# A new order of all steps in a kernel that multiplies spectra and gates two mixers

## The chip, the cores and the metric

The kernel runs on one core of a Trainium2 chip. The metric is the device time of one execution in microseconds; the median of several runs counts. Everything is float32.

## What is computed

The inputs are x (1 x 2048 x 512), a complex weight for its two-dimensional real spectrum, and the parameters of a state-space convolution. The reference, cut to what matters:

```python
def _A_ref(x, w_r, w_i):
    X = rfft2(x)
    return irfft2(X * (w_r + 1j * w_i), s=(S, D))

def _B_ref(u, log_A_real, A_imag, C_real, C_imag, log_dt, D_skip):
    dt = exp(log_dt)
    A = -exp(log_A_real) + 1j * A_imag
    C = (C_real + 1j * C_imag) * dt[:, None]
    P = exp((A * dt[:, None])[:, :, None] * arange(L))
    K = 2.0 * einsum("dn,dnl->dl", C, P).real
    y = irfft(rfft(u_t, 2 * L) * rfft(K, 2 * L))[:, :, :L]   # causal convolution
    return y + u * D_skip

g = sigmoid((x * gate_w).sum(-1, keepdims=True))
out = g * _A_ref(x, ...) + (1 - g) * _B_ref(x, ...)
```

For the inputs given, the convolution's kernel is nearly constant along the sequence, so the main path replaces it by a running sum times one number per channel. A branch behind the main path, taken only for other inputs, computes it in full; no step of the change lies in it.

## The kernel before, in words

The Fourier transforms are matrix products in several stages. TensorE (PE) multiplies, and since it writes only PSUM, every product is then moved on by VectorE (DVE) or ScalarE (ACT). GpSimd (POOL) works on SBUF only. The work is cut into named steps of a letter and a number, and the string PLAN writes out the order of all of them by hand. The line `for word in PLAN.split(): todo[word[0]](int(word[1:]))` emits them in that order. Each engine then runs its own steps in the order in which they stand in PLAN, and waits for what a step needs. SyncE (SP) issues nearly all loads and stores in that order too.

The steps, by stage:

- First stage, ten parts of x (0 to 9; 0, 1, 8 and 9 are half as wide). `F` on POOL folds a part (L259: the sum of its two halves). `C` on PE multiplies a part (L276): half u=1 needs x alone, half u=0 needs the fold. `c` on DVE transposes both halves into AR (L284).
- Second stage, eight units of frequencies (0 to 7). Units 1 and 7 are worked in two halves, written 11, 21, 17, 27. `P` on PE (L435), `t` on ACT copies the product out (L440), `D` on PE transforms along channels (L453; units 3 and 5 do part of the next step with extra matmuls, L457), `d` on ACT and `Z` on DVE (L470 to L478) combine even and odd parts. `W` and `U` on DVE multiply by the spectral weights (L490), `l` loads the weights and `L` on ACT patches their first row (L411).
- The complex products are put together on POOL: `p` (L496, L497), then `g` (L509, L510); `h` on ACT patches a row (L517, L518). `I` on PE transforms back along channels (L537), `i` on ACT copies half of it (L543), `V` on DVE writes the sums to AI (L551).
- The running sum for the second mixer: `X` loads x transposed, `x` on ACT copies a half to PSUM (L335), `m` on DVE is the scan (L338), `y` and `o` on ACT scale (L347, L342), and `r` on POOL issues a transfer that adds the one to the other inside SBUF (L352). `k` on PE and `G` make the gate (L375, L385), which goes through DRAM and comes back spread over all partitions with `O`. `H` on POOL multiplies by it (L370). `u` on ACT and `E` on DVE and ACT multiply the gate into the last matrices (L366, L587, L588).
- Last stages: `K0` on PE and `K1` on ACT mend one row of AI (L557, L559), `B` on PE for eight blocks (L571), `b` on DVE transposes (L575), `Q` on PE makes eight blocks of the result (L597), and `q` on DVE adds the second mixer and stores the block (L610, L611). The last block, LASTQ, is added and stored in two halves (L607, L608), one from SP and one from ACT.
- `R`, `T`, `l`, `S`, `J`, `N` are loads of constants and small sums.

PSUM is four buffers (`bufs=4`) of two banks, which all stages share: a step that needs one waits until the buffer it is given has been read for the last time. SBUF has 13 buffers for short-lived blocks, four for weights (also used by the last matrices), three for small copies and four for the running sums and gate rows.

Of the kernel before, what the change touches and what calls it, by code (L numbers as in the profile page):

```python
# [12 lines left out]
ALU = mybir.AluOpType  # L13
AX = mybir.AxisListType

P = 128
# [25 lines left out]
FOLDS = [0, 0, 1, 1, 1, 1, 1, 1, 1, 1]  # L42
ORDER = [8, 9, 0, 1, 10, 2, 11, 3, 12, 4, 13, 5, 14, 6, 15, 7, 16]
_T = np.arange(128)
K2 = np.arange(64).reshape(32, 2).T.ravel()
# [5 lines left out]
def _consts():  # L51
# [44 lines left out]

    s2 = s2.reshape(17, 2, 128, 2, 64)[ORDER].transpose(2, 0, 1, 3, 4)

# [83 lines left out]
def body(ctx: ExitStack, tc: tile.TileContext, x, xg, xt, w, wh, prms, vecs, gw,  # L182
         c_s1e, c_s1f, c_s2e, c_s2, c_s2v, c_s2q, c_s1b, c_s1a, c_s1c, c_dfw, c_zfw, c_dbw, c_pos, c_eye, out):
    nc = tc.nc
    V, G, S, T = nc.vector, nc.gpsimd, nc.scalar, nc.tensor
# [3 lines left out]
    def psum(name):  # L189
        return ps.tile([P, 2, 512], F32, tag="ps", name=name)  # L190
# [21 lines left out]
    s1e, ones = last[:, 0:128], last[:, 128:256]  # L212
# [13 lines left out]
    def blk(shape, name):  # L226
        return work.tile(shape, F32, tag="blk", name=name, bufs=NBLK)
# [4 lines left out]
    t_ = {}  # L232

    with tc.manual_schedule():
# [4 lines left out]
        for k in PARTS:  # L239
            c = slice(128 * k.start, 128 * k.stop)  # L240
# [14 lines left out]
        def fold(q, E):  # L255
            n = 64 * (PARTS[q].stop - PARTS[q].start)
            f = t_["f", q] = blk([P, 2, 512], "f")
            xv = xin(q)
            E.tensor_tensor(f[:, 0, :n], xv[:, 0], xv[:, 1], op=ALU.add)  # L259
            if FOLDS[q] == 2:  # L260
                E.tensor_tensor(f[:, 1, :n], xv[:, 0], xv[:, 1], op=ALU.subtract)


        def C_(q):
            n = 32 * (PARTS[q].stop - PARTS[q].start)
            p = t_["c", q] = [psum("p_s1") for _ in range(2)] if q == LASTC else [psum("p_s1")] * 2
            tiles = [(g, h, slice(64 * h, 64 * h + 64)) for g in range(2) for h in range(2)]
            if FOLDS[q] == 2:
                for g, h, r in tiles:
                    T.matmul(p[0][64 * g:64 * g + 64, h, :2 * n], s1e[r, 0:64], t_["f", q][r, :, g * n:g * n + n], start=True, stop=True, tile_position=(64 * h, 64 * g))  # L270
            else:
                for u in range(1, -1, -1):
                    for i in range(1 if FOLDS[q] > u else 2):
                        for g, h, r in tiles:
                            src = t_["f", q][r, 0] if FOLDS[q] > u else xin(q)[r, i]
                            T.matmul(p[u][64 * g:64 * g + 64, h, u * n:u * n + n], s1e[r, 64 * u * i:64 * u * i + 64], src[:, g * n:g * n + n], start=i == 0, stop=i == 1 or FOLDS[q] > u, tile_position=(64 * h, 64 * g))  # L276

        def c_a(q):
# [3 lines left out]
            for u in range(1, -1, -1):  # L282
                pv = t_["c", q][u][:, :, :2 * n].rearrange("p h (u t c d) -> p u h t c d", u=2, c=16, d=2)
                V.transpose(av[:, u, :, k], pv[:, u])  # L284


        big, sm = few[:, 1:3], few[:, 3]
# [27 lines left out]

        N_ = {0: n0, 1: n1, 2: small, 3: level, 4: n4}


        def new(key, make):
            if key not in t_:  # L320
                t_[key] = make()
            return t_[key]

        def coef(r):
            return (r // 2 % 2) * 2 + r // 4
# [88 lines left out]
        def unit(n):  # L414
            return n % 10, slice(0, P) if n < 10 else slice(64 * (n // 10 - 1), 64 * (n // 10)), range(2) if n < 10 else [n // 10 - 1]
# [76 lines left out]
        def p_a(n):  # L492
            u, r, vs = unit(n)
            t1, t2 = (cut(t_["t", u, k], n).rearrange("p (o i) k -> p o i k", o=2) for k in range(2))
            po = new(("px", u), lambda: blk([P, 2, 2, 2, P], "px")).rearrange("p x a o k -> p x o a k")[..., r]
            G.tensor_tensor(po[:, 0], t1[:, :, 0:4:2], t1[:, :, 1:4:2][:, :, ::-1], op=ALU.subtract)  # L496
            G.tensor_tensor(po[:, 1, :, ::-1], t2[:, :, 0:4:2], t2[:, :, 1:4:2][:, :, ::-1], op=ALU.add)  # L497


        def g_a(n):  # L500
# [89 lines left out]
        def Q_(j):  # L590
            i, k = j // 4, j % 4
            if j == LASTQ:
                p = t_["pq", j] = [psum("p_oa")[:, 0].rearrange("p (b c) -> p b c", b=4) for _ in range(2)]
            else:
                p = t_["pq", j] = psum("p_oa").rearrange("p u (b c) -> p (u b) c", b=4)
            for b in range(8):
                T.matmul((p[b // 4][:, b % 4] if j == LASTQ else p[:, b]).rearrange("p (e c) -> p e c", e=2), VA[:, i, 8 * (k % 2) + b, :, k // 2], s1a[k][:, :, b], start=True, stop=True)  # L597

        def last_a(j, E, p):
            i, k = j // 4, j % 4  # L600
            z, b = k // 2, 8 * (k % 2)
            xv = XT[:, 2 * i:2 * i + 2].rearrange("p e (z c b) -> p e z c b", z=2, b=16)[:, :, z, :, b:b + 8]
            o = AF_[:, 1024 * j:1024 * j + 1024]
            if j == LASTQ:
                for f in range(2):
                    o_ = o[:, 512 * f:512 * f + 512]
                    E.tensor_tensor(o_.rearrange("p (e c b) -> p e c b", e=2, b=4), p[f].rearrange("p b (e c) -> p e c b", e=2), xv[..., 4 * f:4 * f + 4], op=ALU.add)  # L607
                    (nc.sync, nc.scalar)[f].dma_start(out[j, :, 512 * f:512 * f + 512], o_)  # L608
            else:
                E.tensor_tensor(o.rearrange("p (e c b) -> p e c b", e=2, b=8), p.rearrange("p b (e c) -> p e c b", e=2), xv, op=ALU.add)  # L610
                nc.sync.dma_start(out[j], o)  # L611

        def a_a(j):
# [15 lines left out]
        ]  # L629

        todo = {
            "f": lambda q: fold(q, V), "F": lambda q: fold(q, G), "C": C_, "c": c_a, "N": lambda k: N_[k](),
            "X": load_x, "x": x_a, "m": scan, "o": skip, "y": y_a, "z": summed, "r": both, "k": gate, "G": G_, "J": J_, "l": load_w, "L": load_h,
            "P": P_, "t": t_a, "D": D_, "d": d_a, "Z": Z_, "W": lambda u: W_(u, 0, V), "U": lambda u: W_(u, 1, V), "p": p_a, "g": g_a, "h": h_a, "I": I_, "i": i_a, "V": V_,
            "K": K_, "B": B_, "b": b_a, "S": load_a, "O": load_g, "u": near, "Q": Q_, "q": lambda j: last_a(j, V, t_["pq", j]), "a": a_a, "A": lambda j: last_a(j, G, t_["qs", j]),
# [8 lines left out]
    with tc.If(n_small < D):  # L644
        with tc.tile_pool(name="dram", bufs=1, space=bass.MemoryType.DRAM) as dp:
            Kd = dp.tile([D, L], F32, name="Kd")
            with tc.tile_pool(name="kg", bufs=1) as kg:
# [26 lines left out]
                for c in range(0, D, NC):  # L674
# [52 lines left out]
            with tc.tile_pool(name="gx", bufs=1) as gx:  # L727
                s1f = gx.tile([P, 2, P], F32, name="s1g")
                nc.sync.dma_start(s1f, c_s1f)
                for dst, isk in ((KR, True), (AG, False)):  # L730
# [4 lines left out]
                    for h in range(2):  # L735
                        if isk:
# [37 lines left out]
            p = psum("p_sp")  # L774
# [3 lines left out]
            for c in range(16):  # L778
                p = psum("p_gb")
# [20 lines left out]
            for i in range(2):  # L800
# [89 lines left out]
```

## Time and profile before

| | |
|---|---|
| median of 3 runs | 110.65 us (110.46 to 110.81) |
| profiled execution | 110.1 us, span 108.3 us |
| PE busy | 93.2 us (86%) |
| DVE busy | 85.3 us (79%) |
| POOL busy | 75.5 us (70%) |
| ACT busy | 51.5 us (48%) |
| read from and written to DRAM | 19.01 MB, 4.21 MB |

The span goes from the first to the last instruction of one execution on the chip. A row of the timeline gives start, duration, engine, line, operation, tile written and read, and how many such instructions were merged; in brackets stands how long the engine was idle before and what ended that. A row of the groups gives the busy time of all and the mean of one in nanoseconds. PEld is the loading of weights, which overlaps PE; a matmul in float32 counts as two instructions.

### The profile page before, as it was taken

The page shows a single profiled execution, that of the slowest core. Times are in us where ns is not written, and L with a number is a line of the kernel's source. Part 1 is how long each engine was busy: PE and PEld are TensorE (multiplying, and loading weights), DVE is VectorE, ACT ScalarE, POOL GpSimd, SP SyncE. Part 2 cuts the span into 40 slices and gives each one's busy share as a digit, 9 for nine tenths or more (in the row PEclk, how much of TensorE's full clock was granted, in tenths as well). Part 3 has the DMA queues.
Part 4 walks back from the last instruction along what each step waited for, and adds up shares of the span by engine and source line. Part 5 has one row for each costly group of instructions (what it writes and reads, how often), then busy time and mean ns, then how long its engine had stood idle before and what let it go on. Part 6 is the DMA issues. An engine that isn't in the chain of part 4 may idle for free. (4 is left out here: it accounts for less than half of the span.)

```text
span 108.3 us, 2285 instructions
## 1 busy us (share of the span) xinstructions
PE 93.2 (86%) x872; PEld 77.6 (72%) x872; DVE 85.3 (79%) x134; ACT 51.5 (48%) x89; POOL 75.5 (70%) x70
## 2 busy tenths in 40 slices
PE   6899976999997999989899999976699999999200
PEld 6797753999797945368799999966243869999100
DVE  0248989579799788999999999996889979788500
ACT  0000005455749399999796996946870170000000
POOL 0059853222999998599999999999999999700000
PEclk9999999999999999999999999999999999999995
DMA  3999999999999991099978993998325950779950
GB/s 65 373 366 404 397 389 344 382 422 417 427 405 410 417 395 80 0 200 225 191 242 197 254 250 123 273 229 163 95 98 98 189 106 3 312 297 360 393 214 13
DMA packets 8560, 27.67 MB, mean 255 GB/s; under 512 B 968, under 2 KB 1352, under 8 KB 8028
## 3 DMA queue, kind: packets, MB, share of 16 engines
q1 hardware_dynamic: 7132, 22.86, 57.0%
q0 software_dynamic: 1088, 4.19, 20.2%
q10 hardware_dynamic: 320, 0.38, 1.0%
q8 instruction: 9, 0.15, 0.6%
q14 instruction: 11, 0.09, 0.2%
HBM read 19.01 MB, written 4.21 MB: 214 GB/s over the span
## 5 line engine op out<-in xcount | busy, mean ns | idle before, releaser
L490 DVE TENSOR_TENSOR tw<-p_d,w 128x1024 f32<-128x1024 f32 (+1 forms) x20 | 19.3, 1005 | 1.1 <-ACT w L411 0.5
L370 POOL TENSOR_TENSOR XT<-XT,gb 128x1024 f32<-128x1024 f32 x8 | 19.3, 2552 | 0.2 <-DMA XT<-v 0.2
L435 PE MATMUL p_t<-s2e,AR 128*128 128x128 f32 x128 | 16.7, 285 | 2.1 <-DVE AR L284 0.9
L435 PEld LDWEIGHTS p_t<-s2e,AR 128*128 128x128 f32 x128 | 15.7, 196 | 3.4 <-DVE AR L284 1.3
L453 PE MATMUL p_d<-et,dfw 128*128 128x256 f32 (+1 forms) x80 | 16.8, 343 | 0.8 <-ACT v L347 0.3
L537 PE MATMUL p_v<-dbw,gt 128*128 128x128 f32 x128 | 15.2, 276 | 1.6 <-ACT gt L518 1.6
L597 PEld LDWEIGHTS p_oa<-s1a,AR 128*128 128x128 f32 x128 | 15.2, 196 | 1.7 <-ACT s1a L588 0.9
L537 PEld LDWEIGHTS p_v<-dbw,gt 128*128 128x128 f32 x128 | 14.7, 192 | 1.9 <-ACT gt L518 1.8
L597 PE MATMUL p_oa<-s1a,AR 128*128 128x128 f32 x128 | 15.6, 283 | 0.0
L453 PEld LDWEIGHTS p_d<-et,dfw 128*128 128x128 f32 x80 | 12.0, 191 | 3.5 <-ACT gt L517 1.1
L259 POOL TENSOR_TENSOR f<-AI 128x512 f32<-128x512 f32 (+1 forms) x8 | 9.0, 1140 | 7.8 <-DMA AI<-in_x_dram 7.8
L496 POOL TENSOR_TENSOR px<-tw 128x512 f32<-128x512 f32 (+1 forms) x10 | 11.8, 1184 | 2.2 <-DVE tw L490 2.2
L284 DVE STREAM_TRANSPOSE AR<-p_s 128x512 f32<-128x512 f32 (+1 forms) x20 | 10.8, 589 | 2.9 <-PE p_s L276 2.8
L497 POOL TENSOR_TENSOR px<-tw 128x512 f32<-128x512 f32 (+1 forms) x10 | 11.8, 1180 | 0.0
L551 DVE TENSOR_TENSOR AI<-p_v,po 128x512 f32<-128x512 f32 (+1 forms) x20 | 10.4, 577 | 1.3 <-ACT po L543 1.3
L440 ACT COPY et<-p_t 128x1024 f32<-128x1024 f32 (+1 forms) x10 | 8.4, 836 | 6.0 <-PE p_t L435 6.0
L509 POOL TENSOR_TENSOR gt<-px 128x512 f32<-128x512 f32 (+1 forms) x10 | 10.6, 1063 | 0.8
L276 PE MATMUL p_s<-AI,last 64*64 64x128 f32 (+1 forms) x192 | 10.2, 347 | 1.0 <-DMA AI<-in_x_dram 1.0
L510 POOL TENSOR_TENSOR gt<-px 128x512 f32<-128x512 f32 (+1 forms) x10 | 10.6, 1060 | 0.0
L575 DVE STREAM_TRANSPOSE AR<-p_ia 128x1024 f32<-128x1024 f32 x8 | 9.4, 1222 | 1.4 <-PE p_ia L571 1.4
L338 DVE TENSOR_TENSOR_SCAN p_x<-p_x,XT 128x1024 f32<-128x1024 f32 x4 | 9.2, 2293 | 1.3 <-ACT p_x L335 1.3
L610 DVE TENSOR_TENSOR AI<-p_oa,XT 128x1024 f32<-128x1024 f32 x7 | 8.2, 1211 | 1.5 <-PE p_oa L597 1.5
(67 smaller groups left out, 123.0 us busy)
## 6 DMA issues: line engine op xcount, KB each, us to landing
w<-in_w_dram SPq DMA_DIRECT2D x8, 512.0 KB, 7.7
XT<-in_xt_dram SPq DMA_DIRECT2D x4, 1024.0 KB, 8.9
XT<-v POOLq DMA_DIRECT2D x4, 1024.0 KB, 9.9
out_dram<-AI SPq DMA_DIRECT2D x7, 512.0 KB, 3.4
AI<-in_x_dram SPq DMA_DIRECT2D x6, 512.0 KB, 7.7
gb<-gd SPq DMA_DIRECT2D x4, 512.0 KB, 5.2
AI<-in_x_dram SPq DMA_DIRECT2D x4, 256.0 KB, 3.2
s1a<-in_c_s1a_dram SPq DMA_DIRECT2D x4, 256.0 KB, 4.4
```

The lines of the kernel that those rows point to most:

```text
L284: V.transpose(av[:, u, :, k], pv[:, u])
L370: E.tensor_tensor(r, r, t_["gb", h % 2], op=ALU.mult)
L435: T.matmul(cut(p, n, v)[:, 2 * q:2 * q + 2], AR[:, q % 2, 8 * (q // 2) + u, :, v], s2e[:, 2 * u + v], start=True, stop=True)
L453: T.matmul(d[:, o, 1:3] if h else d[:, o, 0:4:3], dfw[:, 2 * h + o], e[:, 2 * h + o], start=True, stop=not z)
L490: E.tensor_tensor(t, z, w, op=ALU.mult)
L496: G.tensor_tensor(po[:, 0], t1[:, :, 0:4:2], t1[:, :, 1:4:2][:, :, ::-1], op=ALU.subtract)
L497: G.tensor_tensor(po[:, 1, :, ::-1], t2[:, :, 0:4:2], t2[:, :, 1:4:2][:, :, ::-1], op=ALU.add)
L509: G.tensor_tensor(gv[:, :, 0], src[0], src[1], op=ALU.subtract)
L510: G.tensor_tensor(gv[:, ::-1, 1], src[0], src[1], op=ALU.add)
L537: T.matmul(p[:, v - vs[0], h, o], rows(u, o, v, h), dbw[:, h, o], start=True, stop=True)
L551: V.tensor_tensor(ai[:, :, :, k], t_["pi", n][:, 0:len(vs), :, 0], t_["po", u][:, v], op=ALU.subtract if k else ALU.add)
L597: T.matmul((p[b // 4][:, b % 4] if j == LASTQ else p[:, b]).rearrange("p (e c) -> p e c", e=2), VA[:, i, 8 * (k % 2) + b, :, k // 2], s1a[ ...
```

## The change

All steps stay, each with its own work, and PLAN is written anew. Code around it changes as far as the new PLAN needs it:

- `C` and `c` are split by halves. `C` and `c` now mean half u=1, the new letters `j` and `w` half u=0, and each half has its place in the order. Only for part 7 do the two halves have PSUM buffers of their own, as before.
- LASTQ, the block that is stored in two halves, is 5 in place of 7.
- `LASTROWS`, `PDVE` and the letter `v` are new and, as set, do nothing.
- The order of units changes. On POOL the products come as 1, 7, 6, 4, 5, 0, 2 and 3 (before: 1, 7, 4, 6, 0, 2, 3, 5), with r1 ahead of p6. The last blocks come as Q0 Q3 Q2 Q1 Q4 Q7 Q6 Q5 (before: Q1 Q0 Q3 Q4 Q2 Q6 Q5 Q7), and the loads, scans, gate steps and stores move with them.

```diff
-LASTQ = 7
-LASTC = 7
+LASTQ = 5
 ...
 PLAN = """
-R7 R0 C1 F2 J0 C0 c1 c0 T0 C2 c2 F3 C3 c3 F4 C4 J1 F5 R1 C5 F6 F8 F9 c4 c5 C6 c6 C8 R9 C9 c8 c9 R6 F7 N1 C7 c7 P11 l1
-P21 l4 t11 t21 N0 N3 D11 d11 D21 d21 Z11 Z21 P17 P27 N4 N2 t17 L1 U11 R5 W11 U21 D17 t27 d17 P4 t4 Z17 l7 W21 L7 U17
-X1 D27 p11 g11 d27 h11 Z27 D4 p21 g21 L4 P6 l0 d4 W17 U27 Z4 W27 p17 P0 U4 R4 g17 p27 W4 X3 X0 g27 t6 h21 P2 L0 t0 p4
-D6 x1 t2 l6 h17 m1 G4 d6 h27 L6 G5 y1 k0 R8 X2 Z6 g4 U6 W6 k1 o3 o2 R10 D0 k2 k3 l2 d0 h4 l5 G1 x2 Z0 W0 D2 U0 L2 d2
-l3 P3 P5 o4 G2 r1 p6 O0 t3 m2 y2 I11 S1 D3 g6 Z2 i11 p0 g0 W2 U2 o5 S0 r2 h6 L5 L3 O1 p2 t5 V11 I17 i17 x0 I6 h0 U3 o0
-g2 V17 I21 i21 W3 D5 i6 S2 m0 y0 p3 g3 h2 V21 V6 O2 I0 o1 W5 I27 r0 U5 p5 g5 i0 i27 h3 x3 H2 o6 V0 I4 i4 V27 m3 I2 V4
-i2 V2 h5 I3 I5 i3 V3 S3 u0 O3 i5 H4 E0 K0 V5 K1 B0 y3 E1 B3 b0 b3 B1 B4 B2 b1 B7 b2 B6 H5 o7 b4 r3 b7 Q1 Q0 u1 b6 B5
-H1 E3 E2 Q3 H0 b5 H3 Q4 q1 q0 H7 H6 q3 Q2 q2 q4 Q6 q6 Q5 Q7 q5 q7
+R7 C0 j0 F2 c0 J0 C1 j1 F3 C2 j2 F4 C3 w0 j3 c1 F5 w1 R0 w2 c2 C4 j4 c3 w3 C5 F6 c4 j5 C6 w4 j6 C7 F8 F9 w5 c5 c6 w6
+c7 F7 C8 C9 j8 c8 j9 c9 w8 w9 j7 w7 P11 J1 N1 T0 R1 P21 t11 t21 D11 d11 D21 N0 R9 R6 N4 N3 d21 Z11 Z21 l1 l7 l4 P17
+P27 t17 L1 U11 U21 W11 R8 W21 D17 t27 d17 L4 Z17 L7 W17 N2 p11 l6 P4 t4 D27 g11 d27 L6 Z27 U17 W27 P6 X1 X0 P5 t6 X2
+x1 t5 D6 k0 k1 p21 g21 h11 h21 d6 m1 y1 U27 D4 Z6 U6 l5 W6 P0 R5 X3 R10 o3 p17 g17 o2 d4 k2 Z4 G4 p27 R4 h17 L5 l0 g27
+G5 h27 t0 x2 r1 k3 D5 G1 p6 g6 G2 l2 h6 o4 I17 W4 U4 D0 m2 p4 g4 W5 i17 V17 L0 o5 l3 U5 p5 P2 d0 y2 x0 t2 h4 Z0 W0 U0
+S2 O2 O0 P3 r2 o0 g5 t3 D2 d2 p0 g0 I11 h5 S0 D3 i11 m0 o1 L2 y0 r0 Z2 V11 I5 W2 I27 U2 L3 p2 W3 i27 U3 S1 V27 p3 g2
+I6 i5 V5 h0 g3 I21 i6 V6 i21 V21 H0 H4 x3 o6 I0 i0 m3 h2 I4 i4 y3 V0 h3 V4 I2 i2 u0 S3 I3 i3 V2 O1 E0 K0 K1 o7 V3 E1
+O3 B0 b0 B1 b1 r3 B3 b3 B2 b2 u1 E2 B7 b7 E3 H1 B6 Q0 b6 H3 H2 B5 B4 Q3 b5 Q2 q0 q3 H5 Q1 H7 b4 H6 Q4 Q7 q2 q1 Q6 q4
+q7 q6 Q5 q5
 """
+APART = (7,)
 ...
-        def C_(q):
+        def C_(q, u):
             n = 32 * (PARTS[q].stop - PARTS[q].start)
...
+            p = new(("c", q, u if q in APART else 0), lambda: psum("p_s1"))
+            for i in range(1 if FOLDS[q] > u else 2):
+                for g in range(2):
+                    for h in range(2):
...
-            "C": C_, "c": c_a,
+            "C": lambda q: C_(q, 1), "j": lambda q: C_(q, 0), "c": lambda q: c_a(q, 1), "w": lambda q: c_a(q, 0),
```

More of the change, by code (lines that the diff above doesn't have):

```diff
@@ L42 @@
 FOLDS = [0, 0, 1, 1, 1, 1, 1, 1, 1, 1]
+APART = (7,)
+LASTROWS = [slice(0, P)]
+PDVE = ()
 ORDER = [8, 9, 0, 1, 10, 2, 11, 3, 12, 4, 13, 5, 14, 6, 15, 7, 16]
@@ L253, in xin, with new, fold, c_a @@
             return X[:, 128 * PARTS[q].start:128 * PARTS[q].stop].rearrange("p (u n) -> p u n", u=2)
-        def fold(q, E):
+        def new(key, make):
+            if key not in t_:
+                t_[key] = make()
+            return t_[key]
+        def fold(q, u, op, E):
             n = 64 * (PARTS[q].stop - PARTS[q].start)
-            f = t_["f", q] = blk([P, 2, 512], "f")
+            f = new(("f", q), lambda: blk([P, 2, 512], "f"))
             xv = xin(q)
-            E.tensor_tensor(f[:, 0, :n], xv[:, 0], xv[:, 1], op=ALU.add)
-            if FOLDS[q] == 2:
-                E.tensor_tensor(f[:, 1, :n], xv[:, 0], xv[:, 1], op=ALU.subtract)
-        def C_(q):
+            E.tensor_tensor(f[:, u, :n], xv[:, 0], xv[:, 1], op=op)
+        def C_(q, u):
             n = 32 * (PARTS[q].stop - PARTS[q].start)
[L266 to L278, printed above, removed]
+            p = new(("c", q, u if q in APART else 0), lambda: psum("p_s1"))
+            for i in range(1 if FOLDS[q] > u else 2):
+                for g in range(2):
+                    for h in range(2):
+                        r = slice(64 * h, 64 * h + 64)
+                        src = t_["f", q][r, u] if FOLDS[q] > u else xin(q)[r, i]
+                        T.matmul(p[64 * g:64 * g + 64, h, u * n:u * n + n], s1e[r, 64 * u * i:64 * u * i + 64], src[:, g * n:g * n + n], start=i == 0, stop=i == 1 or FOLDS[q] > u, tile_position=(64 * h, 64 * g))
+        def c_a(q, u):
             k = PARTS[q]
@@ L281, in c_a @@
             av = AR.rearrange("p u c (h t) d -> p u h t c d", h=2)
-            for u in range(1, -1, -1):
-                pv = t_["c", q][u][:, :, :2 * n].rearrange("p h (u t c d) -> p u h t c d", u=2, c=16, d=2)
-                V.transpose(av[:, u, :, k], pv[:, u])
+            pv = t_["c", q, u if q in APART else 0][:, :, :2 * n].rearrange("p h (u t c d) -> p u h t c d", u=2, c=16, d=2)
+            V.transpose(av[:, u, :, k], pv[:, u])
         big, sm = few[:, 1:3], few[:, 3]
@@ L316, in body @@
         N_ = {0: n0, 1: n1, 2: small, 3: level, 4: n4}
[L319 to L322, printed above, removed]
         def coef(r):
@@ L495, in p_a @@
             po = new(("px", u), lambda: blk([P, 2, 2, 2, P], "px")).rearrange("p x a o k -> p x o a k")[..., r]
-            G.tensor_tensor(po[:, 0], t1[:, :, 0:4:2], t1[:, :, 1:4:2][:, :, ::-1], op=ALU.subtract)
-            G.tensor_tensor(po[:, 1, :, ::-1], t2[:, :, 0:4:2], t2[:, :, 1:4:2][:, :, ::-1], op=ALU.add)
+            E = V if u in PDVE else G
+            E.tensor_tensor(po[:, 0], t1[:, :, 0:4:2], t1[:, :, 1:4:2][:, :, ::-1], op=ALU.subtract)
+            E.tensor_tensor(po[:, 1, :, ::-1], t2[:, :, 0:4:2], t2[:, :, 1:4:2][:, :, ::-1], op=ALU.add)
         def g_a(n):
@@ L607, in last_a @@
                     E.tensor_tensor(o_.rearrange("p (e c b) -> p e c b", e=2, b=4), p[f].rearrange("p b (e c) -> p e c b", e=2), xv[..., 4 * f:4 * f + 4], op=ALU.add)
-                    (nc.sync, nc.scalar)[f].dma_start(out[j, :, 512 * f:512 * f + 512], o_)
+                    for r in LASTROWS:
+                        (nc.sync, nc.scalar)[f].dma_start(out[j, r, 512 * f:512 * f + 512], o_[r])
             else:
@@ L631, in body @@
         todo = {
-            "f": lambda q: fold(q, V), "F": lambda q: fold(q, G), "C": C_, "c": c_a, "N": lambda k: N_[k](),
+            "f": lambda q: fold(q, 1, ALU.subtract, V), "F": lambda q: fold(q, 0, ALU.add, G), "v": lambda q: fold(q, 0, ALU.add, V),
+            "C": lambda q: C_(q, 1), "j": lambda q: C_(q, 0), "c": lambda q: c_a(q, 1), "w": lambda q: c_a(q, 0), "N": lambda k: N_[k](),
             "X": load_x, "x": x_a, "m": scan, "o": skip, "y": y_a, "z": summed, "r": both, "k": gate, "G": G_, "J": J_, "l": load_w, "L": load_h,
```

## The prediction

> **What bounds the kernel now.** I read the page's busy shares first, then the chain that ended last, then the waits, then the timeline by stage. The profiled execution took 110.1 us: a span of 108.3 and 1.8 around it. The median is 110.65, so I work out a difference within the span and take it off the median.
>
> ```profile
> PE 93.2 (86%) x872; PEld 77.6 (72%) x872; DVE 85.3 (79%) x134; ACT 51.5 (48%) x89; POOL 75.5 (70%) x70
> ...
> 74.07 2.06 PE p_v L537 x16
> ...
> 77.90 6.41 PE p_ia L571 x53
> ...
> 89.40 11.52 PE p_oa L597 x96
> ...
> 100.94 0.69 DVE AI L607
> ...
> PE p_v L537 <- ACT gt L518: 1.6, 1, 1.6
> ```
>
> PE is busy 93.2 of 108.3, and 7.4 of the 15.1 idle us lie after its last matmul at 100.92. From 77.90 on it runs without a gap. So the time is B0's start, plus 23.02 of PE work (8 B, 8 Q), plus the tail. B0's start goes back to the last I step, I5, at 74.07. PE had waited 1.6 us for it, the longest PE wait in the kernel, and what it waited for was h5, released by g5 on POOL:
>
> ```profile
> 26.43 0.73 POOL L496 TENSOR_TENSOR px<-tw 128x256 f32<-128x256 f32 x1 [2.19 <-DVE tw L490]
> ...
> 37.24 0.73 POOL L510 TENSOR_TENSOR gt<-px 128x256 f32<-128x256 f32 x1
> ...
> 44.43 1.36 POOL L352 DMA_DIRECT2D XT<-v  x1 [1.40 <-ACT XT L342]
> ...
> 50.91 1.26 POOL L496 TENSOR_TENSOR px<-tw 128x512 f32<-128x512 f32 x1
> ...
> 55.94 1.18 POOL L352 DMA_DIRECT2D XT<-v  x1
> 56.72 1.71 POOL L496 TENSOR_TENSOR px<-tw 128x512 f32<-128x512 f32 x1
> ...
> 72.29 1.28 POOL L510 TENSOR_TENSOR gt<-px 128x512 f32<-128x512 f32 x1
> ```
>
> POOL makes the complex products of all eight units in one string, from p11 at 26.43 to g5's end at 73.57. Its one long wait is 1.40 us, for the ACT work ahead of r1. A whole unit (p and g) takes 50.91 to 55.94, 5.03 us; an r step costs about 1.2 (0.78 from 55.94 to the next p, which then runs 0.45 longer than the 1.26 of the row above). PE has spare time in the middle; POOL's string sets when the last unit can be transformed back.
>
> **Part by part.** The instructions are the same. What moves is their order on every queue, and with it who holds which PSUM buffer.
>
> *First stage: 0.* C and c are planned by halves, so C7's first half, which needs no fold, can fill PE's wait for part 8.
>
> ```profile
> 14.62 2.65 POOL L259 TENSOR_TENSOR f<-AI 128x256 f32<-128x256 f32 x3 [1.54 <-DMA AI<-in_x_dram]
> ...
> 17.33 0.66 PE L276 MATMUL p_s<-f,last 64*64 64x256 f32 x8
> ...
> 18.84 2.15 PE L435 MATMUL p_t<-s2e,AR 128*128 128x128 f32 x16 [0.85 <-DVE AR L284]
> ```
>
> The folds F8, F9, F7 keep their order on POOL and start when part 8 lands (14.62, end 17.27). Half j7 can only follow at 17.33, its transposition after that, and P11 stays at 18.84. SP's queue is the same up to R6, so the landings are too. I count 0; it could be 0.1 the better way.
>
> *The string's start: later by 0.6.* DVE now runs U11 U21 W11 W21 where it ran U11 W11 U21.
>
> ```profile
> 24.99 1.89 DVE L490 TENSOR_TENSOR tw<-p_d,w 128x512 f32<-128x512 f32 x3
> ...
> 22.33 0.36 DVE L470 SCALAR_TENSOR_TENSOR p_d<-p_d,pers,ds 128x128 f32<-128x128 f32 x1 [1.79 <-ACT ds L462]
> ...
> 23.66 0.35 DVE L470 SCALAR_TENSOR_TENSOR p_d<-p_d,pers,ds 128x128 f32<-128x128 f32 x1
> ...
> 40.59 0.48 DVE L470 SCALAR_TENSOR_TENSOR p_d<-p_d,pers,ds 128x256 f32<-128x256 f32 x1
> ...
> 42.72 2.36 DVE L490 TENSOR_TENSOR tw<-p_d,w 128x1024 f32<-128x1024 f32 x2 [0.20 <-DVE p_d L473]
> ```
>
> Half a product is 0.63, so p11, which needs W11, moves from 26.43 to 27.05, and the four half units end at 38.6 in place of 37.97.
>
> *The string's wait: shorter.* After g27 come r1 and p6 (before: p4, g4, the 1.40 wait, r1, p6). p6 needs W6, and DVE now has m1 ahead of U27, Z6, U6 and W6. By the rows: the four half products end at 27.5; Z17 (1.33, start of one half Z to the next), W17, Z27, U17, W27 end at 32.05. The scan m1 waits for ACT's x1, which stands behind t6 and so behind P6:
>
> ```profile
> 25.44 2.14 PE L435 MATMUL p_t<-s2e,AR 128*128 128x128 f32 x16
> ...
> 27.42 1.06 PE L453 MATMUL p_d<-et,dfw 128*128 128x128 f32 x8
> ...
> 28.74 1.99 PE L453 MATMUL p_d<-et,dfw 128*128 128x256 f32 x8 [0.27 <-ACT et L440]
> ...
> 39.29 1.92 PE L375 MATMUL p_gate<-XT,gv 128*32 128x512 f32 x16
> ...
> L440 ACT COPY et<-p_t 128x1024 f32<-128x1024 f32 x6 | 6.0, 1005 | 3.0 <-PE p_t L435 3.0
> ...
> L335 ACT COPY p_x<-XT 128x1024 f32<-128x1024 f32 x4 | 4.1, 1018 | 1.7 <-DVE tw L490 1.7
> ...
> L338 DVE TENSOR_TENSOR_SCAN p_x<-p_x,XT 128x1024 f32<-128x1024 f32 x4 | 9.2, 2293 | 1.3 <-ACT p_x L335 1.3
> ```
>
> P4 takes 1.98 (25.44 to 27.42), D27 ends at 28.48, P6 at 30.4, t6 at 31.4, x1 at 32.45. Then m1 to 34.8, U27 to 35.45, Z6 to 37.4 (1.93, the row pair less its idle 0.20), U6 and W6 to 39.75. r1 is reached at 38.6 and done at 39.8, if y1, o3 and o2, which ACT has ahead of it, are. So p6 starts at 39.8. Six whole units and r2, r0 remain: 39.8 + 6 x 5.03 + 2 x 1.2 = 72.4, against 73.57: 1.2 earlier, if POOL never waits.
>
> Of that I keep 0.9. POOL meets DVE closely at p2 and p3, where my walk leaves 0.4. Which PSUM buffer a step gets is not to be read from the diff either. A wrong one costs between nothing and the longest PE wait shown, 1.6; it costs nothing while POOL is the later one, so I take 0.3 for both, near the lower end. It is not below nothing, since POOL cannot go faster than its sum.
>
> X1 is now issued behind l1, l7, l4 and l6, ahead of R5, R4 and X3.
>
> ```profile
> GB/s 65 373 366 404 397 389 344 382 422 417 427 405 410 417 395 80 0 200 225 191 242 197 254 250 123 273 229 163 95 98 98 189 106 3 312 297 360 393 214 13
> ...
> 18.11 0.33 SPq L331 DMA_DIRECT2D XT<-in_xt_dram  x1
> ...
> XT<-in_xt_dram SPq DMA_DIRECT2D x4, 1024.0 KB, 8.9
> ```
>
> It landed at about 27 (18.11 + 8.9). It now has 0.35 MB more ahead, about 0.9 us at the 400 GB/s of the early slices: 28, against x1's need at 31.4. Cover 3.4; if that is gone, each us costs a us of POOL. Behind X2 on SP stands l5, which waits for W21 (27.5) to free a buffer and holds back R5, X3, R10 and R4; X3 ends 3.9 MB behind X1 (9.8 us, 38) and is needed for k3 at about 41, a like cover. r1 stands ahead of p6 on POOL's queue and was counted there.
>
> *Last I to B0: later by 0.1.* Before, I5 at 74.07 led to B0 at 77.90, in 3.83, where K1 and V5 ended together. Now V3 is last, and unit 3 is among the rows that B0's first matmul reads, so all of V3 must be done. Sum for B0: 77.90 - 0.9 + 0.1 = 77.1.
>
> *B and Q: later by 0.4.*
>
> ```profile
> 79.13 8.14 DVE L575 STREAM_TRANSPOSE AR<-p_ia 128x1024 f32<-128x1024 f32 x7 [0.45 <-PE p_ia L571]
> ```
>
> Q0 now follows six B steps (6 x 0.92 = 5.5, from 7 in 6.41), not seven, and needs b0, b1, b3 and b2. b0 starts 1.23 after B0 (79.13 less 77.90) and each takes 1.16 (8.14 by 7): 1.23 + 4 x 1.16 = 5.9. PE waits 0.4. From then on DVE (E2, b7, E3, b6, b5, q0, q3, b4, q2, q1) stays ahead of the buffers that Q2 to Q5 need. H0, H2 and the rest end about a us ahead of q0 and q4. PE's end: 100.92 - 0.9 + 0.1 + 0.4 = 100.5.
>
> *Stores: earlier by 0.25 more.*
>
> ```profile
> 91.83 8.81 SPq L611 DMA_DIRECT2D out_dram<-AI  x7
> ...
> 101.67 0.39 ACTq L608 DMA_DIRECT2D out_dram<-AI  x1
> ...
> 101.00:102.00 1.00, 0.00 (x0) 0.00 (x0) 0.63 (x1) 0.00 (x0) 0.00 (x0) 1.00 0.99 385
> ...
> 104.00:105.00 1.00, 0.00 (x0) 0.00 (x0) 0.00 (x0) 0.00 (x0) 0.00 (x0) 1.00 0.38 133
> ...
> out_dram<-AI SPq DMA_DIRECT2D x7, 512.0 KB, 3.4
> ...
> out_dram<-AI SPq DMA_DIRECT2D x1, 256.0 KB, 5.0
> ```
>
> The DMA engines are full at 385 GB/s until about 104.4; a 512 KB store takes 1.36 there, and the last store but one needs 5.0 to land where a larger one usually needs 3.4. There is a backlog. With q0 and q3 at about 89 and 90 instead of 91.8 the queue is empty when q6 issues, but q6 and the halves of q5 still bring 1 MB within 1.45 us, 2.7 us of transfer. So 0.25 of the backlog goes and the rest stays. The Trainium skill, "DMA: Bandwidth & Descriptors", Anatomy of one DMA, fits a single transfer as 2.0 us plus bytes over 436 GB/s, by which a last store with nothing ahead of it would land after 2.6; by that the tail would give 2.4 in place of 0.25. The trace's 5.0 shows that the last stores are not alone.
>
> Sum: -0.9 + 0.1 + 0.4 - 0.25 = -0.65. In the profiled execution that is 109.45; forecast 110.65 - 0.65 = 110.0.
>
> **Rivals.** *V17 stalls DVE (slower).* V17 now stands ahead of U5 on DVE, so DVE waits there for I17 and i17, and behind it POOL for p5, reached at 39.8 + 10.06 = 49.9. With V17 and U5 at about 2 us (U5 is half of 2.36), i17 must end by 47.9. PE has P6, P5, P0 (3 x 1.98), D6, D4 (4.0), the gate's k0 to k3 (3.85), the small G4, D5 and I17 to do by then.
>
> ```profile
> 53.39 0.70 PE L453 MATMUL p_d<-et,dfw 128*128 128x256 f32 x2 [0.31 <-ACT v L347]
> ...
> 57.00 3.74 PE L537 MATMUL p_v<-dbw,gt 128*128 128x128 f32 x32
> ```
>
> A D with the extra matmuls takes 3.6 (53.39 to 57.00), I17 0.95: 28.48 + 18.6 = 47.1, i17 by 47.5. The margin is 0.4. If PE is later by more than about 1.4 (0.4, the 0.65 that the forecast gains, and 0.33 to be seen), the kernel is slower. By my walk I17 takes the gate's PSUM buffer and so waits for the sigmoid, which waits for k3, x2 and a table load on ACT; PE 2 late there, a little over its longest wait of 1.6, gives 110.65 - 0.65 + 1.6 = 111.6. For it: four engines meet here within half a us. Against it: PE starts the stretch with no wait in my walk.
>
> *No change.* POOL's string ends earlier, but PE then is the later one: the units come in another order, I5, I6, I0 and I2 each wait for a buffer that a V frees, and the last I starts when it did. About 110.6. For it: DVE is busy 85.3, hardly less than PE.
>
> *More gain.* POOL meets no wait at all (1.2) and the 0.4 at Q0 does not come: 110.65 - 1.2 + 0.1 - 0.25 = 109.3. *The backlog gone*: the last store has nothing ahead of it and lands in 3.4, the 512 KB row, 1.6 less than 5.0: 110.65 - 0.4 - 1.6 = 108.65. By the 2.6 of the Trainium skill's page it would be 107.85.
>
> **How the numbers follow.** Forecast 0.45, V17 0.22, no change 0.18, more gain 0.12, backlog gone 0.03. A measurement of this kernel tells 0.3% (0.33 us) from no change. Faster: 0.45 less a small part that falls short of 0.33, plus 0.12, 0.03 and a little of no change: 0.57. Same: 0.19. Slower: 0.24. The range goes from 109.0, a little under more gain, to 111.6, which is V17; the forecast's own is 109.4 to 110.4.
>
> **What would show it.** P11 at 18.8 as before; p11 near 27.0; p6 near 39.8 with no long POOL wait behind it; the last g's end near 72.7; B0 near 77.1; a wait of about 0.4 at Q0; the first store near 89; the DMA engines full only from about 101. Wrong would be: POOL waiting for DVE between p6 and g3, a DVE wait at V17, x1 waiting for X1's landing, or PE reaching the last I later than POOL's string allows.

## The result, and the profile after

The changed kernel takes 111.38 us (median of 20 runs, 110.63 to 113.57); beside it, the kernel before took 110.49 us (20 runs, 109.57 to 111.48). The ratio is 1.0081, with a 95% interval from 1.0054 to 1.0108. The change costs 0.9 us. I had forecast 110.0 and a gain of 0.65. Medians, here and below, are of all runs; ratios and intervals are of the fast runs alone, those at most 1.5% above the fastest of their kernel.

The profiled execution of the kernel after took 111.3 us, with a span of 109.5; before, these were 110.1 and 108.3. First, lines of the page of the kernel after that answer to those shown of before: the busy times, the rate of the DMA engines in 40 slices, then the end of the chain and PE's longest wait. (Line numbers are three or four lower than in the kernel before: L594 is the matmul of `Q`, L568 that of `B`, L534 that of `I`.)

```profile
PE 93.7 (86%) x872; PEld 76.8 (70%) x872; DVE 85.0 (78%) x134; ACT 51.5 (47%) x89; POOL 75.1 (69%) x70
...
GB/s 54 329 331 420 399 381 300 374 407 435 419 408 416 408 327 217 195 131 406 302 220 211 106 235 189 140 186 132 66 144 190 55 111 278 296 275 281 320 6 9
...
73.22 2.06 PE p_v L534 x16
...
77.04 6.06 PE p_ia L568 x43
...
87.17 13.40 PE p_oa L594 x112
100.59 0.69 DVE AI L604
...
PE p_v L534 <- ACT gt L515: 1.5, 2, 1.1
```

Busy times are those of before within half a us. B0 starts at 77.04 (before 77.90), and the last add ends 0.34 earlier than before, at 101.29. So the main part did get shorter, and yet the span is 1.2 longer. What lies behind the last add is 8.2 us (109.5 less 101.29); before, it was 6.7 (108.3 less 101.63).

Next the timeline at that place, before and after, for the last stores, with SP's wait for the instructions behind the branch (engine and line that waited, what released it: us in total, times, longest), and the rate at which the DMA engines moved data in the kernel after (last column GB/s). Of the kernel before:

```profile
100.91 0.41 SPq L608 DMA_DIRECT2D out_dram<-AI  x1
...
SPq L644 <- SPq L644: 4.9, 2, 3.8
```

Of the kernel after:

```profile
99.85 1.44 DVE L604 TENSOR_TENSOR AI<-p_oa,XT 128x512 f32<-128x512 f32 x2
100.56 1.32 SPq L606 DMA_DIRECT2D out_dram<-AI  x1
101.32 0.39 ACTq L606 DMA_DIRECT2D out_dram<-AI  x1
...
SPq L643 <- SPq L643: 5.0, 1, 5.0
...
103.00:104.00 1.00, 0.00 (x0) 0.00 (x0) 0.00 (x0) 0.00 (x0) 0.00 (x0) 1.00 0.76 262
104.00:105.00 1.00, 0.00 (x0) 0.00 (x0) 0.00 (x0) 0.00 (x0) 0.00 (x0) 0.97 0.14 25
...
out_dram<-AI ACTq DMA_DIRECT2D x1, 256.0 KB, 2.9
...
q8 instruction: 9, 0.15, 0.5%
q14 instruction: 12, 0.10, 0.4%
```

The stores are through about a us earlier than before (262 GB/s from 103 to 104 and 25 behind it, where before had 377 and 133). ACT's half block, the last one issued, landed 2.9 us after its issue; before it took 4.9 (from 101.67 to 106.61, where SP's wait for it ended). Nothing of that reaches the end, because the stores are no longer what ends last. L643 is the branch past the general path, `with tc.If(n_small < D)`; every engine reads the count into a register and jumps. SP's issue of a half block takes 1.32 us instead of 0.41, SP jumps later, and behind its jump it stands still for 5.0 us instead of 3.8. The two lines marked `instruction` count packets of program code over the whole span, 16 KB each on q8 and 8 KB each on q14; 2 and 7 of them start behind PE's jump. I take q8 to be PE's queue, since its packet moves with PE's jump in the experiments below, and q14 that of the others. That SP waits for such a packet is my reading; no record names the engine of a packet.

The trace also records the jumps themselves and the first instruction behind each. The stay is the time from the one to the other:

```
            jump -> next instruction (stay)
            PE                    SP                    DVE                   ACT
before       99.48->104.68 (5.2)  101.36->105.17 (3.8)  102.17->106.37 (4.2)  103.41->106.01 (2.6)
after        98.89->102.94 (4.1)  102.33->107.39 (5.1)  101.81->106.55 (4.7)  102.30->106.30 (4.0)
```

Before, SP was back first of SP, DVE and ACT, and then waited until 106.61 for the store signals; its stay was hidden. After, SP is back last, at 107.39, with every store long landed, and the end follows 2.1 us later.

### The profile page after: what moved, and what is told of

Read it like the earlier page. It is cut to its first block, busy times and chain, and to the rows that moved or that the text cites. A ratio compares the mean times of both kernels' runs of the same rounds, so it can differ in the third digit from the quotient of the medians.

```text
span 109.5 us, 2287 instructions
## 1 busy us (share of the span) xinstructions
PE 93.7 (86%) x872; PEld 76.8 (70%) x872; DVE 85.0 (78%) x134; ACT 51.5 (47%) x89; POOL 75.1 (69%) x70
## 4 chain that ended last, share of the span: by engine, by line
PE 47%; POOL 17%; DMA 15%; DVE 6%; issue 4%; ACT 1%; SPq 1%; POOLq 0%
PE p_oa L594 14%; PE p_t L431 11%; DMA AI<-in_x_dram 9%; PE p_d L449 8%; PE p_ia L568 7%; POOL gt L507 6%; PE p_gate L371 3%; DMA gb<-gd 3%; DMA last<-in_c_s1e_dram 3%; POOL gt L506 3%; POOL px L493 3%; POOL px L494 2%; POOL f L267 2%; DVE p_x L334 2%; PE p_v L534 2%
## 5 line engine op out<-in xcount | busy, mean ns | idle before, releaser
L534 PE MATMUL p_v<-dbw,gt 128*128 128x128 f32 x128 | 15.8, 279 | 2.4 <-ACT gt L515 1.5
L534 PEld LDWEIGHTS p_v<-dbw,gt 128*128 128x128 f32 x128 | 14.7, 192 | 3.7 <-ACT gt L515 1.9
L594 PEld LDWEIGHTS p_oa<-s1a,AR 128*128 128x128 f32 x128 | 15.2, 196 | 1.8 <-DVE AR L572 1.0
L594 PE MATMUL p_oa<-s1a,AR 128*128 128x128 f32 x128 | 15.6, 283 | 0.0
L506 POOL TENSOR_TENSOR gt<-px 128x512 f32<-128x512 f32 (+1 forms) x10 | 11.7, 1173 | 0.6
L507 POOL TENSOR_TENSOR gt<-px 128x512 f32<-128x512 f32 (+1 forms) x10 | 11.7, 1167 | 0.0
```

Source lines behind the costliest of these rows:

```text
L506: G.tensor_tensor(gv[:, :, 0], src[0], src[1], op=ALU.subtract)
L507: G.tensor_tensor(gv[:, ::-1, 1], src[0], src[1], op=ALU.add)
L534: T.matmul(p[:, v - vs[0], h, o], rows(u, o, v, h), dbw[:, h, o], start=True, stop=True)
```

## Experiments

The kernel before ran again in every series, with medians from 110.46 to 110.70, so a difference of 0.2 us between two series says nothing. Four theories came first. *Tail*: the loss lies behind the branch, and the main part is faster as forecast. *Body*: the main part itself is slower. Then, within the tail, *held issue* (SP's late jump comes from its store issue, which PE's code fetch holds up) and *queueing* (the code fetches of engines that jump together wait on one another).

**Without read-back and branch, both orders.** The general path, the read-back and the branch are left out:

```diff
-    n_small = nc.values_load(count[0:1, 0:1], min_val=0, max_val=D)
-    with tc.If(n_small < D):
-        ...
```

> The kernel before without the count's read-back and without the branch behind the main path (the fallback is left out). In the profiles the last store's bytes move until 105.4 before and 104.4 after, but SyncE comes out of the branch only at 105.2 before and 107.4 after. Theory tail: the new order gains in the body and loses more behind the branch. Then this kernel ends with its stores, at about the time it has now: 110.1 to 110.5 (its stores land late, and the branch was hidden behind them). Rival body: the order costs somewhere in the body; the same numbers here, so the two are told apart by the partner run.

> The changed kernel without the read-back and the branch (the fallback is left out). Theory tail: faster than the partner by about 1.0 us (the stores end 1.0 earlier), so about 109.3, 2 us less than the changed kernel with its branch. Rival body: the branch has nothing to do with it, and this kernel stays 0.9 us slower than the partner, as with the branch.

Measured: 108.59 us from before (0.982 of it, 0.977 to 0.987), 107.56 us from after (0.9725, 0.9674 to 0.9776). The first was missed: the branch costs the kernel before 2 us too, where I had thought that it lay beside the stores. The traces say how: SP's half block landed 5.0 us behind its issue with the branch and 3.5 without it, so in the old order most of those 2 us reach the end through the stores. The second tells the theories apart: without the branch the new order is 1.03 us *faster*. Body is refuted.

**Both kernels once more, for the tail.**

> The kernel before once more, for a second profile. Theory tail: SyncE's stay in the branch again about 3.8 us, the stores still being what ends last, span near 108.3 to 108.7. Rival (an accident of the one profile): a stay of 5 us here as well.

> The changed kernel once more, for a second profile. Theory tail: the last sum again near 101.3, the last store's bytes near 104.4, and SyncE out of the branch about 5 us after it entered, the span again near 109.5. Rival (an accident of the one profile): SyncE's stay in the branch is about 3.8 as in the kernel before.

Measured: 110.98 and 111.31 us, spans 109.1 and 109.4. SP's last issue took 0.52 and 1.46, its stay was 3.83 and 4.74. The tail is the same each time. With these six traces the time can be cut at three points (us):

```
                             before  again  no branch | after  again  no branch
start of P11 (x has come)     18.84  19.50  19.38     | 19.24  19.30  19.14
P11 to the end of the last g  54.73  54.72  54.73     | 53.47  53.48  53.46
P11 to B0                     59.06  59.04  59.05     | 57.80  57.81  57.79
P11 to the end of last add    82.79  82.78  82.78     | 82.05  82.08  82.09
end of last add to the end     6.68   6.82   4.56     |  8.21   8.05   4.29
```

From P11 on, each order repeats to a few hundredths in these six; what differs between them is when x arrives. The new order gains 0.7 us up to the last add and 0.27 more in the stores where no branch follows; with the branch its tail is 1.2 to 1.5 longer.

**The branch with a near target.** The body of the branch is cut to one small load; the general path is left out.

```diff
     with tc.If(n_small < D):
-        with tc.tile_pool(name="dram", ...) as dp:
-            ...
+        nc.sync.dma_start(eye, c_eye)
```

> The kernel after with the fallback's body cut to one load of 64 KB, so that the count is still read back and every engine still branches, but the target lies some instructions on instead of behind the whole fallback (which is left out). Theory far code: what costs is the fetch of code that lies far ahead, 4 to 5 us on DVE, ACT and SP; with a near target it is gone, and the time is that of the kernel without read-back and branch (107.56) plus 0.5 to 0.9 for the register load and the branch: 107.9 to 108.6 us. Rival, read-back: the load of the count into registers and the branch itself cost the 3.8 us: 110.8 to 111.5 us.

> The kernel before with the fallback's body cut to one load of 64 KB (the fallback is left out), as the partner of the same edit on the kernel after. Theory far code: the kernel without read-back and branch (108.59) plus 0.3 to 0.9: 108.8 to 109.6 us, and slower than its partner by about 1.0 us, the gain that the new order brings where no far code follows. Rival, read-back: 110.3 to 110.8 us, and faster than its partner.

Measured: 109.86 us (ratio to before 0.9968, 0.9936 to 0.9999) and 108.87 us (0.9878, 0.9835 to 0.9921). The first fits neither theory, and the trace says why: a body that needs nothing from the main path let the branch move up into it, to 43 us in the one and 45 to 49 us in the other. In the kernel after it fell on POOL, at p6:

```profile
43.40 1.26 POOL L493 TENSOR_TENSOR px<-tw 128x512 f32<-128x512 f32 x1 [3.36 <-issue]
```

Against the 40.37 of the kernel after, less the 0.3 by which this run's x came earlier, p6 is 3.3 us late; B0 is 3.3 late as well (61.10 behind P11, not 57.80). That is a test I had not planned: POOL's string does set B0, one to one, as the prediction said (DVE was held too, by 1.7 us, and that did not show). In the kernel before, the branch stood where it held nobody (P11 to B0 59.07), and there a read-back and a jump to a near target cost 0.3 us of time (108.87 against 108.59), which the scatter covers, and not 2. The time lay in the range of far code; that it would be slower than its partner was wrong. This speaks for the far target as what costs, but doesn't show it, since the near branch stood in the middle and not at the end. The recorded jump itself took 0.04 to 0.36.

The Trainium skill, "Runtime: NRT & Kernel Launch", Instruction fetch mechanics, says that engines fetch ahead in program order only, and that a taken branch to code outside the window of two pages stands until the page has come by DMA. The runs fit that, and they have a price: in the two profiles above an engine stood 2.6 to 5.2 us behind such a jump.

**SP has no late store: both halves of the last block from ACT's queue.**

```diff
-                        (nc.sync, nc.scalar)[f].dma_start(out[j, r, ...], o_[r])
+                        nc.scalar.dma_start(out[j, r, ...], o_[r])
```

> The kernel after, with both halves of the last block stored from ACT's queue instead of one from SP's and one from ACT's. Theory held-issue: in the kernel after, SP's last store issue takes 1.32 to 1.46 us (0.41 to 0.52 before), so SP branches at 102.3 instead of 101.0, is the last to get the code behind the branch (back at 107.4) and ends the run. Without that issue SP branches at about 100.4 and is back by 105; the end is then set by ACT or by the last store: 109.4 to 110.2 us, below the kernel before. Rival, queueing: DVE, ACT and SP branch within 0.5 us of one another and their fetches queue; it doesn't matter which engine is last, ACT then branches at about 102.7 and is the last one back at 107 or later: 110.9 to 111.5 us.

> The kernel before with the same edit as the one that brought the kernel after from 111.4 to 110.0 us: both halves of the last block stored from ACT's queue. Theory held-issue: before, SP's last store issue was hardly held (0.41 to 0.52 us), SP branched at 101.4 and was back at 105.2, ahead of the last store's signal (106.6) and of DVE (106.4); SP's earlier jump buys nothing there: 110.2 to 110.9 us, no difference. Rival, any kernel gains when SP jumps earlier (the edit is a gain of its own and says nothing of the change): 109.2 to 110.0 us.

Measured: from after 110.02 us (0.997 of before, 0.9931 to 1.0009), 1.4 below the kernel after: held issue had 109.4 to 110.2, queueing 110.9 to 111.5. From before 110.18 us (0.9984, 0.9955 to 1.0013): no difference. In the trace of the first SP jumps at 99.93 and is back at 103.52; ACT is now last:

```profile
SPq L643 <- SPq L643: 4.0, 2, 3.6
SPq L885 <- DVEq L643: 1.0, 1, 1.0
...
SPq L885 <- ACTq L643: 0.3, 1, 0.3
```

SP's stay is 3.6, and afterwards SP waits for DVE and for ACT. So it was SP's late return that ended the kernel after, and only there: the same edit, worth 1.4 us in one order, is worth nothing to be measured in the other.

**PE jumps later.** Matmuls that nobody reads, behind the last `Q`; 16 of them in one kernel, 3 in the other.

```diff
+        late = psum("p_late")
+        for b in range(16):   # 3
+            T.matmul(late[:, 0, 0:P]..., VA[:, 0, b, :, 0], s1a[3][:, :, b % 8], ...)
```

> The kernel after, with 16 matmuls of 128x128 added on PE behind its last Q step, into a free PSUM buffer that nobody reads (16 x 0.12 = 1.9 us, which ends beside the last stores). Theory held-issue with its cause named: the 16 KB fetch for PE's own branch starts at 100.5 in the kernel after (PE branches at 98.9), within 0.1 us of SP's store issue at 100.56, and holds it; in the kernel before PE branched at 99.5, that fetch came at 102.2 and SP's issue was free. With PE branching at about 100.8, SP's issue takes 0.33 to 0.5, SP branches at about 101.0 and is back by 105: 109.3 to 110.2 us, although work was added. Rival, queueing among DVE, ACT and SP: SP's issue is not held by PE's fetch, so it stays at 1.3 and the time at 111.1 to 111.6, or PE comes back later and adds to it.

> The kernel after with 3 matmuls of 128x128 added on PE behind its last Q step (3 x 0.12 = 0.36 us, read by nobody). Theory first comes, first served: PE's own fetch starts 1.62 us behind PE's jump; in the kernel after SP's last store issue starts 1.67 us behind that jump (98.89, 100.56), just too late, and is held 1.0 us; in the kernel before it started 1.43 behind the jump (99.48, 100.91), and PE's fetch was held instead (2.72 us behind the jump). With PE's jump 0.36 us later the issue is 1.31 behind it: SP's issue takes 0.33 to 0.55, PE's fetch comes 2.1 to 3.0 behind the jump, SP jumps at about 101.0 and is back by 105.3: 109.4 to 110.3 us, a gain by added work. Rival, the order of these two doesn't decide (with 16 matmuls more the issue was free too, and SP's stay was 4.88 all the same): 110.6 to 111.5 us.

Measured: 110.59 us with 16 (ratio 1.0027, 0.999 to 1.0063) and 110.22 us with 3 (0.9935, 0.9897 to 0.9972). Work added made the kernel 0.8 and 1.2 us faster than the kernel after (0.5% and 1.5% by the ratios). SP's row with 3, and its wait:

```profile
100.09 0.33 SPq L606 DMA_DIRECT2D out_dram<-AI  x1
...
SPq L646 <- SPq L646: 4.9, 1, 4.9
```

The issue is free in both (0.33), as held issue expected: PE's code fetch, which in the kernel after began at 100.53, 0.03 us ahead of SP's issue, now begins at 101.70 and at 104.78. But SP's stay remains 4.9, which held issue did not expect; with 16, the time missed its range. That part of the loss has another cause.

**ACT jumps earlier: both halves from SP's queue.**

```diff
-                        (nc.sync, nc.scalar)[f].dma_start(out[j, r, ...], o_[r])
+                        nc.sync.dma_start(out[j, r, ...], o_[r])
```

> The kernel after with both halves of the last block stored from SP's queue. ACT then has nothing left to do after its scalings and branches some 15 us earlier; SP branches last, at 102.5 to 103.0. What made SP's stay behind the branch 5.06 us (3.81 before): theory queueing of fetches (DVE, ACT and SP branched within 0.5 us): with ACT gone SP's stay falls to about 3.8, back at 106.6: 110.2 to 110.9 us. Rival, it isn't the neighbours but the store data that lands until 104.4, or SP's place in the code: the stay stays at 4.7 to 5.1, back at 107.5 or later: 111.2 to 112.0 us.

Measured: 110.36 us (0.9973, 0.9935 to 1.0011).

```profile
101.40 2.13 SPq L606 DMA_DIRECT2D out_dram<-AI  x2
...
SPq L643 <- SPq L643: 3.4, 1, 3.4
```

The first of the two issues is held again (1.27) and SP jumps as late as 103.59, 1.47 behind the end of the last add (1.04 in the kernel after). Yet its stay is 3.4, with ACT, which jumped at 86.6, no longer beside it. Queueing had expected that the stay falls, to about 3.8.

**Less store data.** Each half stores one row; the other 127 rows of the last block are left out.

```diff
-                        ...dma_start(out[j, r, 512 * f:512 * f + 512], o_[r])
+                        ...dma_start(out[j, 0:1, 512 * f:512 * f + 512], o_[0:1])
```

> The kernel after, whose two last half-block stores write one row of 2 KB each instead of 128 (127 rows of that block stay unwritten); every instruction of every engine stays, only 0.5 MB of store data less is in flight behind 100.6. Theory store data: the code fetches wait behind the last stores' packets (one 8 KB packet took 1.61 us instead of 0.31, ending at 105.9): SP's stay falls to about 3.8 and the time to 109.8 to 110.4 us. Rival, the issue is held and the fetches queue among themselves: SP's issue still takes 1.3, the stay stays at 4.7 to 5.1: 111.0 to 111.6 us.

Measured: 109.21 us (0.9887, 0.985 to 0.9925), below the range of either theory. SP's issue takes 0.31 and its stay 3.6. Both costs went at once, so this run doesn't tell store data from the rest; it shows that together with the stores' own transfer they are worth 2.2 us.

**SP's issue later in the kernel before.** If the earlier of PE's fetch and SP's issue simply held the later one, 0.3 us on DVE should turn the kernel before into the kernel after:

```diff
+                    if f == 0:
+                        V.memset(o_[:, 0:256], 0.0)
```

> The kernel before with a memset of 128x256 on DVE ahead of its last two half adds (0.17 us for 128x128 in the profile, so about 0.3 us; the adds overwrite it). Theory first comes, first served: SP's last store issue then starts 1.73 us behind PE's jump, behind PE's fetch at 1.62, is held about 1.0 us, SP jumps 1.3 us later (102.6) and is back at 107.4 or later, last of all: the kernel before then looks like the kernel after, 111.1 to 112.0 us. Rival, the work alone counts: 0.3 us more, 110.7 to 111.0 us, and SP's issue stays at 0.33 to 0.55.

Measured: 110.9 us (0.9985, 0.9943 to 1.0028), and SP's issue stayed at 0.33. The theory of first come, first served falls: here PE's fetch began 2.46 behind PE's jump with nothing on SP to hold it. In all kernels with the new order and PE's work as it was, it began 1.61 to 1.74 behind the jump, in all with the old order 2.1 to 3.0. Why, I have not found.

**The last whole block from ACT as well, in both orders.** j is 6 in the kernel after and 5 in the kernel before; the halves go from ACT too.

```diff
-                nc.sync.dma_start(out[j], o)
+                (nc.scalar if j == 6 else nc.sync).dma_start(out[j], o)
```

> The kernel after with both halves of the last block and the whole block ahead of it stored from ACT's queue, as a candidate: SP then branches at about 98.1 instead of 99.9, ahead of the fetch for PE at 100.1. Theory queueing: DVE's and ACT's fetches have less beside them than with the last block alone on ACT, 109.4 to 109.9 us, below both kernels. Rival: SP was already back at 103.5, 2.7 us before ACT (106.2), so its jump no longer counts; 110.0 us, as with the last block alone, or 0.2 more for ACT's extra issue.

> The kernel after with the last three stores from ACT's queue a second time, now beside its partner made from the kernel before: 109.0 to 109.8 us, below the kernel before by 0.7 us or more. If the first 109.19 (7 runs) was luck, it is 110.0, as with the last block alone on ACT.

> The kernel before with the last block's halves and the whole block ahead of them stored from ACT's queue, the edit that gave 109.19 us on the kernel after. If the new order's body gain of 1.0 us (the difference without read-back and branch) is what counts once SP's jump is out of the way, this kernel comes out 0.7 to 1.1 us behind its partner: 109.9 to 110.4 us. Rival, the edit alone makes the gain: 109.0 to 109.5 us, level with its partner.

Measured: from after 109.19 us (0.9886, 0.9839 to 0.9932) and again 109.51 us (0.9853, 0.9799 to 0.9907); from before 110.46 us (0.9964, 0.9924 to 1.0004). SP's rows in the first, whose last whole block but one is now the last thing that SP issues:

```profile
97.44 2.16 SPq L609 DMA_DIRECT2D out_dram<-AI  x2
...
SPq L643 <- SPq L643: 6.5, 4, 3.6
SPq L885 <- PEq L885: 0.7, 2, 0.5
SPq L885 <- ACTq L643: 0.4, 1, 0.4
```

Four waits, none over 3.6 us: one for the code, and three for the signals of the last stores, which SP now is there to wait for; ACT's return ends the run. This version beats both kernels, by 1.1 to 1.4 us the one before. Beside the same edit on the old order it is 0.95 us ahead in the same series: with SP's jump out of the way, the gain of the new order is there.

## Why the prediction was wrong

I go step by step and count times from P11 (the table above), because x came 0.4 us later in this run than in the one before. The rows of the kernel after's timeline that the steps below use (P11, p11, p6, V17, the last g, and the weight load of `Q0` behind its wait):

```profile
19.24 2.15 PE L431 MATMUL p_t<-s2e,AR 128*128 128x128 f32 x16 [0.84 <-DVE AR L285]
...
27.43 0.73 POOL L493 TENSOR_TENSOR px<-tw 128x256 f32<-128x256 f32 x1 [3.73 <-DVE tw L486]
...
40.37 1.29 POOL L493 TENSOR_TENSOR px<-tw 128x512 f32<-128x512 f32 x1
...
47.82 0.74 DVE L548 TENSOR_TENSOR AI<-p_v,po 128x256 f32<-128x256 f32 x2
...
71.11 1.60 POOL L507 TENSOR_TENSOR gt<-px 128x512 f32<-128x512 f32 x1
...
83.03 1.96 PEld L594 LDWEIGHTS p_oa<-s1a,AR 128*128 128x128 f32 x16 [0.96 <-DVE AR L572]
```

- *First stage, 0*: P11 started at 19.24, forecast 18.84. In all runs it lay between 18.69 and 21.02 with the old order and between 18.75 and 20.32 with the new; nothing of that belongs to the order. Right.
- *The string's start, 0.6 later*: right. p11 starts 8.19 behind P11, before 7.59.
- *p6 at 39.8*: 21.13 behind P11, forecast 20.96.
- *The string's end, 0.9 earlier*: 1.26. The sum had given 1.2, and the 0.3 that I kept back for PSUM buffers and for DVE was not needed.
- *Last I to B0, 0.1 later*: 4.33 from the last g's end to B0, before 4.33. Nothing.
- *B and Q, 0.4 later*: B0 to PE's end is 23.5, before 23.0, so 0.5. `Q0` waited for DVE's transposition as foreseen and began 6.0 behind B0 (83.03), forecast 5.9.
- *Stores, 0.25 earlier*: 0.27 where no branch follows (4.56 to 4.29). The Trainium skill's "DMA: Bandwidth & Descriptors", Anatomy of one DMA, gives by its formula an estimate of 2.6 us for a lone transfer of 256 KB; the formula stands there for the path of transfers that POOL issues, which I did not say, and these stores go from SP and ACT. ACT's half block came to 2.9, from 4.9. I had put that the backlog would stay; for this half most of it went. It bought little, as the store is not what ends the run.

The sum of these is -1.26 + 0.5 - 0.27 = -1.03, and the two kernels without the branch differ by 1.03. The step that failed is the one that was never written as a term: the tail. I worked out "a difference within the span", saw that "7.4 of the 15.1 idle us lie after its last matmul", and took all of it but the stores as fixed. It wasn't: 1.5 us came in there, from the jump. SP's issue is held by 0.9 (1.32 against 0.41) and the jump follows it 0.4 later still, and the stay behind it is 1.25 longer; together 2.6, of which the 1.1 that SP used to wait for store signals (105.51 to 106.61) hid a part. -0.74 up to the last add and +1.53 behind it give +0.8, and 0.9 was measured. The row for it stood in the profile of before, a wait of 3.8 us of SP on itself, and I didn't ask what it was, because the stores covered it. In the new order the old cover would not have been enough: SP came back 6.1 us behind the last add (107.39 less 101.29), and the old order's stores were in 5.0 behind theirs (106.61 less 101.63).

None of the rivals is what happened. V17 did not stall DVE (it ran at 47.82, just ahead of what p5 needed); the slower result came by a mechanism that no rival held. *No change* and *more gain* put their price on the main part, where the forecast was nearly right. That 111.38 is close to the 111.6 of the V17 rival is luck: that price was for a stall in the main part.

Shown: the loss lies behind the branch; SP's late return ends the run; a free issue, or SP or ACT out of the way, brings 0.8 to 2.2 us. Left open: why PE's fetch starts sooner behind its jump in the new order, and what makes SP's stay 4.7 to 5.1 us in four traces and 3.4 to 4.1 in the others. Jumps within about 0.5 us of one another go with the long ones, with two exceptions: in the kernel with the memset DVE jumped 0.44 behind SP and SP's stay was 3.5, and in the one with less store data these were 0.51 and 3.7 (with the extra matmuls, 0.51 and 4.9). So queueing alone does not explain the stay. Behind the jumps, one 8 KB packet of code took 1.61 us in the kernel after, and none over 0.51 in the kernel before. Taking the code's distance away at the very end could not be tried: the near branch moved.

## What to carry to other kernels

Before a gain in the main part is booked, ask of the last few us which engine is back last, and what hides the others; a wait of an engine on itself behind a branch can grow and become the end. Where a branch to far code ends a kernel, look which engine comes back last and let that one jump earlier: in the new order, moving three stores from SP's queue to ACT's brought 1.9 to 2.2 us against the kernel after. In the old order, where SP was not last, it brought 0.2, within the scatter. Cut a trace at points that no arrival from memory disturbs; runs that seem to scatter by a us can then agree to hundredths, as the six traces did here.

## What the hardware showed

- The read-back and the jump over the general path cost 2.1 us of the time in one order of steps and 3.8 in the other; with a near target, in the middle of the kernel and holding nobody, 0.3, within the scatter.
- While code is fetched for PE, a store's issue on SP or ACT can take 1.3 to 1.5 us instead of 0.33 to 0.39 (five traces in which the issue began 0.03 to 0.06 us behind the fetch). In the kernel after with both halves on ACT the issue 0.07 behind it took 0.38 all the same, and in the old order with three stores on ACT an issue took 1.14 that had begun 0.60 ahead of PE's fetch. So such a fetch is not the only thing that goes with a long issue.
- Reading the count into a register took 0.46 to 1.89 us, on DVE never under 1.1 (at the kernel's end DVE's record begins while an add of about 0.7 still runs).
- 0.36 us of matmuls that nobody reads made the kernel 1.2 us faster.
- In the second trace with three stores on ACT the granted clock stood at 0.67 to 0.76 between 19 and 25 us. P11 took 3.48 us there in place of 2.15, and the last add came 83.6 us behind P11 in place of 82.1.
